# GpSimd's product y and its lower parts of the q and k units, each made as two half-width operations

## The chip, the cores and the metric

The kernel runs on one core of one Trainium2 chip. The core has a matrix engine (TensorE, PE in the profile, with its weight loads as PEld), a vector engine (VectorE, DVE), an activation engine (ScalarE, ACT), GpSimd (POOL), and SyncE (SP), which issues most DMAs. Each engine runs its own instruction list in order, and engines wait for each other through semaphores. The metric is device time in microseconds (us), the median of several runs.

## The reference

Three layers follow each other: attention with a top-32 mask, a gated channel mixer with a causal convolution, and a token mixer with a learned phase. What matters here is the attention:

```python
scores = scale * np.matmul(q, k.transpose(0, 1, 3, 2))      # 4 batches, 8 heads, 576 x 576
kth = np.partition(scores, -32, axis=-1)[..., -32:-31]
mask = scores >= kth
scores = np.where(mask, scores, -1e9)
attn = softmax(scores)                                       # written out in the reference
out = np.matmul(attn, v)                                     # head_dim 64
```

The later layers are matrix products of 512 x 512 and 576 x 576 with elementwise work between them. All is float32.

## The kernel before

**Tiles and steps.** The scores are cut into 144 tiles of 128 query rows by 576 keys. One step of the main loop advances a pipeline of tiles: TensorE makes the scores of a later tile, ScalarE moves them out of PSUM (`scores_out`, L572), VectorE finds the largest 24 of each row (`pick`, eleven short operations on L594, L598, L600), and the 25th to 32nd are found through a product that GpSimd makes.

**The path of y.** For tile i, ScalarE makes n, the sign of each score against the 24th largest (`count`, L607), with its row sum in acc. GpSimd multiplies scores by n into y (`below`, L615, 576 columns) and appends eight numbers made from acc (L616, 8 columns). VectorE takes the eight largest of y (`rest`, L621), and one of them is the threshold in `thrs`. ScalarE makes the exponentials e (`expo`, L202), and VectorE masks, multiplies and sums them in one operation with two SBUF inputs (`mask`, L676, called "the mask" below). The masked tile is then turned by TensorE and multiplied with v.

**Buffers.** There is one buffer for y: y of the next tile waits until L621 has read this one. There are two for n: n of tile i-1 (in step i) needs the buffer that y of tile i-3 (made in the same step) has read.

**q and k units.** For each pair of heads (a unit) ScalarE rounds k and q to the high part (`split_high`, L247), and GpSimd subtracts it to leave the low part (`split_low`, L253): one operation for k over 576 columns, one for q over 576, 320 or 256 columns. DMAs (`double`, L262 to L270) then copy both parts to the places where TensorE reads them.

**Other GpSimd work.** L630 (`nmax`, 6 columns, every third tile), L732 (row sums of a unit), L837 (a sum in the convolution of batches 1 to 3, whose result VectorE needs on L845), L415 (low parts of the later layers, here X, G and L), L354 (weights). On VectorE, L340, L341 and L335 belong to the weights, and L415 makes low parts there too.

**What sets the order.** VectorE and ScalarE run in the order in which the Python code records their work (`FIXED`, `manual_schedule`): one step records the names of `STEP` in turn, among them `rest`, `below`, `pick`, `mask`. The lists of TensorE, GpSimd and SyncE are ordered by the framework's scheduler, which works from its own estimates.

Of the kernel before, what the change touches and what calls it, by code (L numbers as in the profile page):

```python
# [11 lines left out]
F32 = mybir.dt.float32  # L12
# [5 lines left out]
ALU = mybir.AluOpType  # L18
# [72 lines left out]
def mixer(ctx, tc, qT, kT, vt, w_val, conv_t, w_out, w_theta, w_tok, w_ch, out, flag):  # L91
    nc = tc.nc
    safe = flag is None
    P = 128
    B, S, DM = vt.shape
# [97 lines left out]
    s_tiles, s_psum, groups, xT, gate, W, ms = {}, {}, {}, {}, {}, {}, {}  # L193
    owed = [0.0]
    jobs, later, mid, extras, chains, flowing, fill = [], [], [], [], [], [], []
# [21 lines left out]
    def columns_of(t, x):  # L217
        return slice(*COLS[x]) if t == "q" and x is not None else slice(0, S)
# [30 lines left out]
    def split_low(u, x):  # L249
        for t in "kq":  # L250
            high, low = raws[t, u, x]
            c = columns_of(t, x)
            nc.gpsimd.tensor_tensor(low[:, c], low[:, c].bitcast(F32), high[:, c].bitcast(F32), ALU.subtract)  # L253

    def double(u, j, x):

# [320 lines left out]
    def group(i):  # L577
        g, k = divmod(i, G)
        if g not in groups:
            d = {}  # L580
            for nm, shape in (("cand", [P, G, 8 * NSUB]), ("tops", [P, G, K if safe else KC])):
                d[nm] = wk.tile(shape, F32, tag=nm, name=f"{nm}_{g}", bufs=2 if nm == "cand" else 3)
            groups[g] = d
        return groups[g], k
# [26 lines left out]
    def below(i):  # L611

        d, k = group(i)
        y = wk.tile([P, S + NK], F32, tag="y", name=f"y_{i}")
        nc.gpsimd.tensor_tensor(y[:, :S], s_tiles[i], d.pop(("n", k)), ALU.mult)  # L615
        nc.gpsimd.tensor_tensor(y[:, S:], steps, d.pop(("acc", k)).broadcast_to([P, NK]), ALU.subtract)  # L616
        d["y", k] = y

# [653 lines left out]
    for k, part in enumerate(order):  # L1272
        i0 = part["tiles"][0].i
        u, x = part["u"], part["x"]
        split = u // NP in SPLIT
        if k < 2:
            at(-1, lambda u=u: fetch(u, (nc.sync, nc.sync if u else nc.scalar)))
            for j in range(2):
                at(j if k else -1, lambda u=u, j=j: direct(u, j))
        elif split or x == 0:  # L1280
            when = (i0 - 7, i0 - 5, i0 - 5, i0 - 4, i0 - 3) if split or i0 and order[k - 1]["x"] and order[k - 1]["u"] // NP in SPLIT else (i0 - 9, i0 - 8, i0 - 7, i0 - 6, i0 - 3)
            a = (u, x if split else None)
            for step, do in zip(when, (load_heads, split_high, split_low, *(
                    lambda u, x, j=j: double(u, j, x) for j in range(2)))):
                at(max(step, 0), lambda do=do, a=a: do(*a))
        if split or x == 0:
            at(i0 + VAT[0 if split else 1], lambda part=part: load_v(part))
# [58 lines left out]
    def work_1(i):  # L1346
# [13 lines left out]
        "convert": convert,  # L1360
        "pick": lambda i: i <= N and (by_group(i, group_of) if safe else pick(i)),
        "below": lambda i: None if safe else inside(i - 3, below),
        "scores_out": lambda i: i + AHEAD - 1 in s_psum and scores_out(i + AHEAD - 1),
        "turn_out": lambda i: inside(i - LAG - TO - 1, turn_out),
# [65 lines left out]
```

## Time and profile before

| | us |
|---|---|
| median of 3 runs | 820.15 (819.28 to 820.51) |
| the profiled execution: its own time | 818.77 |
| the profiled execution: span of its instructions | 817.0 |

| engine | busy us of the span | instructions |
|---|---|---|
| TensorE matmuls | 722.8 (88%) | 4478 |
| VectorE | 665.9 (82%) | 2708 |
| ScalarE | 633.6 (78%) | 1517 |
| GpSimd | 451.4 (55%) | 557 |

Busy time of an engine counts an operation from its start to its end as the profile records them, also where it stands still in between. The chain of waits is made by going back from the last instruction, at each step to what released it or to the instruction ahead of it on its engine. It tells which engine held the end at which moment.

### The profile page before, as it was taken

The numbers are of one execution on the slowest core, as the hardware profiler recorded it, in microseconds if no ns is written. First come the engines' busy times: TensorE is split into PE (matmuls) and PEld (weight loads), VectorE is DVE, ScalarE is ACT, GpSimd is POOL, SyncE is SP. The second block draws the span as 40 slices with busy tenths as digits, with TensorE's granted clock in tenths as the row PEclk, the third lists the DMA queues.
The fourth block names the chain that finished last, engine by engine and source line by source line (L and its number), as shares of the span: only waits on it lengthen the run. The fifth ranks groups of instructions, "written<-read, shape, count | busy, mean of one in ns | idle before, by whom it ended". The sixth has DMA issues, their size and how long they took to land.

```text
span 817.0 us, 15416 instructions
## 1 busy us (share of the span) xinstructions
PE 722.8 (88%) x4478; PEld 580.9 (71%) x4478; DVE 665.9 (82%) x2708; ACT 633.6 (78%) x1517; POOL 451.4 (55%) x557
## 2 busy tenths in 40 slices
PE   5467899958999899996989989999999899999995
PEld 3345577536757676965787767788988677898995
DVE  5999999879977899997999799989988795353522
ACT  6788999889779888998789988889988874346411
POOL 5977676556644454657577445647895251015500
PEclk9998999989999999998889999999999999999998
DMA  5676776545342343276365523325662300070002
GB/s 153 169 181 167 188 185 173 153 112 137 77 129 72 78 145 91 61 221 174 91 182 159 170 75 87 73 73 145 181 185 79 104 16 1 1 244 21 2 1 63
DMA packets 69982, 94.33 MB, mean 115 GB/s; under 512 B 13312, under 2 KB 36736, under 8 KB 69888
## 3 DMA queue, kind: packets, MB, share of 16 engines
q1 hardware_dynamic: 69568, 92.82, 41.7%
q8 instruction: 38, 0.62, 0.3%
q14 instruction: 56, 0.46, 0.2%
q10 hardware_dynamic: 320, 0.43, 0.2%
HBM read 49.96 MB, written 13.11 MB: 77 GB/s over the span
## 4 chain that ended last, share of the span: by engine, by line
PE 43%; DVE 30%; ACT 13%; POOL 6%; DMA 4%; issue 3%; SPq 1%; ACTq 0%; POOLq 0%; DVEq 0%
PE px L780 7%; PE py L1134 7%; DVE cand L594 6%; DVE s L676 5%; DVE thrs L621 4%; PE pval L529 4%; PE px2t L529 4%; PE pth L529 4%; PE ph L529 4%; PE py L1153 3%; PE pt L689 3%; DVE gp L845 2%; DVE cand L600 2%; PE ps L558 2%; DVE tops L598 2%
## 5 line engine op out<-in xcount | busy, mean ns | idle before, releaser
L615 POOL TENSOR_TENSOR y<-s,n 128x576 f32<-128x576 f32 x144 | 188.6, 1309 | 191.9 <-DVE thrs L621 139.4
L594 DVE MAX8 cand<-s 128x8 f32<-128x96 f32 x864 | 210.2, 244 | 6.1 <-ACT s L572 6.1
L676 DVE SCALAR_TENSOR_TENSOR s<-s,thrs,e 128x576 f32<-128x576 f32 x144 | 140.8, 978 | 2.3 <-ACT e L202 2.3
L607 ACT ACTIVATE n<-s,tops 128x576 bf16<-128x576 f32 x144 | 112.0, 778 | 32.0 <-POOL y L615 13.5
L572 ACT ACTIVATE s<-ps 128x256 f32<-128x256 f32 (+1 forms) x288 | 103.4, 405 | 25.3 <-PE ps L693 9.3
L1134 PE MATMUL py<-w_tok,z 128*128 128x256 f32 (+1 forms) x432 | 116.1, 408 | 6.4 <-DVE z L990 6.4
L621 DVE MAX8 thrs<-y 128x8 f32<-128x584 f32 x144 | 109.3, 759 | 5.4 <-POOL y L616 4.8
L202 ACT ACTIVATE e<-s,least 128x576 f32<-128x576 f32 x144 | 110.8, 769 | 1.4 <-POOL gp L837 1.3
L689 PE MATMUL pt<-ident,s 128*128 128x128 f32 x576 | 95.1, 286 | 16.9 <-ACT pT L708 8.0
L689 PEld LDWEIGHTS pt<-ident,s 128*128 128x128 f32 x576 | 69.8, 146 | 43.1 <-ACT pT L708 14.7
L558 PE MATMUL ps<-kh_None,q 128*128 128x256 f32 x240 | 91.9, 390 | 5.5 <-ACT rb L759 2.8
L1134 PEld LDWEIGHTS py<-w_tok,z 128*128 128x128 f32 x432 | 77.4, 190 | 26.4 <-DVE z L990 8.8
L708 ACT COPY pT<-pt 128x512 f32<-128x512 f32 x128 | 73.1, 571 | 23.2 <-PE pt L689 13.5
L780 PE MATMUL px<-pT,v 128*64 128x256 f32 (+1 forms) x512 | 76.6, 435 | 13.4 <-ACT pT L708 13.4
L598 DVE MAX8 tops<-cand 128x8 f32<-128x48 f32 x432 | 82.6, 191 | 0.1
L559 PE MATMUL ps<-kl_None,q 128*128 128x256 f32 x240 | 71.8, 302 | 0.0
L780 PEld LDWEIGHTS px<-pT,v 128*64 128x64 f32 x512 | 34.3, 143 | 44.2 <-ACT pT L708 15.7
L558 PEld LDWEIGHTS ps<-kh_None,q 128*128 128x128 f32 x240 | 46.8, 195 | 20.1 <-ACT s L572 6.5
L558 PE MATMUL ps<-kh,q 128*128 128x256 f32 (+1 forms) x80 | 36.0, 457 | 22.2 <-ACT s L572 9.3
L600 DVE MATCH_REPLACE8 cand<-tops,cand 128x48 f32<-128x48 f32 x288 | 55.0, 191 | 0.0
L559 PEld LDWEIGHTS ps<-kl_None,q 128*128 128x128 f32 x240 | 47.4, 198 | 2.3 <-issue 0.5
L697 ACT COPY pT<-ps 64x128 f32<-64x128 f32 (+1 forms) x160 | 39.1, 245 | 11.9 <-PE ps L693 5.6
(206 smaller groups left out, 1716.3 us busy)
## 6 DMA issues: line engine op xcount, KB each, us to landing
kh_None<-kh_None SPq DMA_DIRECT2D x48, 144.0 KB, 2.7
kl_None<-kl_None SPq DMA_DIRECT2D x48, 144.0 KB, 2.8
v<-in_vt_dram SPq DMA_DIRECT2D x20, 256.0 KB, 3.7
out_dram<-x2T SPq DMA_DIRECT2D x16, 256.0 KB, 2.9
w<-ch SPq DMA_DIRECT2D x16, 256.0 KB, 4.4
w<-theta SPq DMA_DIRECT2D x16, 256.0 KB, 5.4
raw_hi<-in_w_tok_dram SPq DMA_DIRECT2D x7, 512.0 KB, 3.9
kh<-kh SPq DMA_DIRECT2D x24, 144.0 KB, 2.4
```

The source lines that it names most:

```text
L202: ins = nc.scalar.activation(out, src, func, **more).ins
L529: nc.tensor.matmul(ps[o : o + n], x, y, start=(i + k == 0), stop=(i == last and k == len(ways) - 1), skip_group_check=(n < P))
L558: nc.tensor.matmul(bank[:, :w], q2, kh[:, lo:hi], start=(j == js[0]), stop=False)
L559: nc.tensor.matmul(bank[:, :w], q2, kl[:, lo:hi], start=False, stop=(j == js[-1]))
L594: nc.vector.max(d["cand"][:, k, 8 * x : 8 * x + 8], s_tiles[i][:, x * SUB : (x + 1) * SUB])
L607: nc.scalar.activation(n, s_tiles[i], AF.Sign, bias=d["tops"][:, k, KC - 1 : KC], scale=-(1.0 + 2.0 ** -22), accum_out=acc)
L615: nc.gpsimd.tensor_tensor(y[:, :S], s_tiles[i], d.pop(("n", k)), ALU.mult)
L621: nc.vector.max(thrs[:, N - 1 - i : N - 1 - i + NK], d.pop(("y", k)))
L676: nc.vector.scalar_tensor_tensor(p, p, thr(i), e.exp, ALU.is_ge, ALU.mult, accum_out=part["sums"][:, e.slot : e.slot + 1])
L689: nc.tensor.transpose(e.pt[:, c, :], p[:, c * P : (c + 1) * P], ident)
L780: nc.tensor.matmul(px[d, :], of_v, pT[:, k, :], start=(c == 0), stop=(c == NF), skip_group_check=True)
L1134: nc.tensor.matmul(ps, z[:, m * P : (m + 1) * P], W["tok"][:, w, lo:hi], start=(i + k == 0), stop=(i == NF))
```

## The change

Both products of GpSimd are cut in the middle of their columns and recorded as two operations behind each other. Nothing else is edited.

```diff
         for t in "kq":
             high, low = raws[t, u, x]
             c = columns_of(t, x)
-            nc.gpsimd.tensor_tensor(low[:, c], low[:, c].bitcast(F32), high[:, c].bitcast(F32), ALU.subtract)
+            mid = (c.start + c.stop) // 2
+            for c in (slice(c.start, mid), slice(mid, c.stop)):
+                nc.gpsimd.tensor_tensor(low[:, c], low[:, c].bitcast(F32), high[:, c].bitcast(F32), ALU.subtract)
...
         y = wk.tile([P, S + NK], F32, tag="y", name=f"y_{i}")
-        nc.gpsimd.tensor_tensor(y[:, :S], s_tiles[i], d.pop(("n", k)), ALU.mult)
+        n = d.pop(("n", k))
+        for c in (slice(0, S // 2), slice(S // 2, S)):
+            nc.gpsimd.tensor_tensor(y[:, c], s_tiles[i][:, c], n[:, c], ALU.mult)
         nc.gpsimd.tensor_tensor(y[:, S:], steps, d.pop(("acc", k)).broadcast_to([P, NK]), ALU.subtract)
```

144 operations on y become 288, and 36 on units become 72. The lists of TensorE, VectorE and ScalarE keep their order. GpSimd's list keeps its order too, with the halves next to each other, but for three places, and SyncE's list has one pair of DMAs exchanged (a copy of a high q part now ahead of the copy of a low k part, in the unit of the second place below). Line numbers from L253 on grow by 2, and those behind L615 by 4.

GpSimd's list of the kernel before at about 137 us of its trace: y of one tile, the two low parts of a unit, then the eight columns that finish y.

```order
L354 TENSOR_TENSOR w_tok<-raw_hi_130 128x512
L615 TENSOR_TENSOR y_1964<-s_1678,n_1850 128x576
L253 TENSOR_TENSOR kl_None<-kl_None,kh_None 128x576
L253 TENSOR_TENSOR ql_None<-ql_None,qh_None 128x576
L616 TENSOR_TENSOR y_1964<-steps,acc_1849 128x8
L630 TENSOR_SCALAR least<-tops_1781 128x6
```

The same place of GpSimd's list in the changed kernel:

```order
L356 TENSOR_TENSOR w_tok<-raw_hi_130 128x512
L619 TENSOR_TENSOR y_2008<-s_1716,n_1891 128x288
L255 TENSOR_TENSOR kl_None<-kl_None,kh_None 128x288 x2
L255 TENSOR_TENSOR ql_None<-ql_None,qh_None 128x288 x2
L619 TENSOR_TENSOR y_2008<-s_1716,n_1891 128x288
L620 TENSOR_TENSOR y_2008<-steps,acc_1890 128x8
L634 TENSOR_SCALAR least<-tops_1821 128x6
```

The second half of y stands behind the whole unit now; before, all 576 columns stood ahead of it.

GpSimd's list of the kernel before at about 373 us: a unit whose k part stands ahead of the y of a tile and whose q part behind it.

```order
L616 TENSOR_TENSOR y_4943<-steps,acc_4883 128x8
L253 TENSOR_TENSOR kl_None<-kl_None,kh_None 128x576
L615 TENSOR_TENSOR y_4992<-s_4735,n_4925 128x576
L616 TENSOR_TENSOR y_4992<-steps,acc_4924 128x8
L253 TENSOR_TENSOR ql_None<-ql_None,qh_None 128x576
```

The same place in the changed kernel:

```order
L620 TENSOR_TENSOR y_5046<-steps,acc_4985 128x8
L255 TENSOR_TENSOR kl_None<-kl_None,kh_None 128x288
L619 TENSOR_TENSOR y_5096<-s_4835,n_5028 128x288 x2
L620 TENSOR_TENSOR y_5096<-steps,acc_5027 128x8
L255 TENSOR_TENSOR kl_None<-kl_None,kh_None 128x288
L255 TENSOR_TENSOR ql_None<-ql_None,qh_None 128x288 x2
```

Only the first half of the k part stands ahead of y now. The third place is at about 433 us, where two operations L (L415, 512 columns) stood behind y: now the first of them stands between the halves of y.

## Rows read from the trace of the kernel before

**Rows 1.** The page: busy time by engine, and the chain's shares by engine.
```profile
PE 722.8 (88%) x4478; PEld 580.9 (71%) x4478; DVE 665.9 (82%) x2708; ACT 633.6 (78%) x1517; POOL 451.4 (55%) x557
PE 43%; DVE 30%; ACT 13%; POOL 6%; DMA 4%; issue 3%; SPq 1%; ACTq 0%; POOLq 0%; DVEq 0%
```

**Rows 2.** Busy time by stretch: stretch, its us, then PE, PEld, DVE, ACT, POOL, clock, DMA.
```profile
285.00:420.00 135.00, 122.88 (x806) 98.90 (x802) 126.12 (x536) 116.18 (x292) 83.22 (x105) 0.94 0.48 136
```

**Rows 3.** One line's instructions, L676 (the mask): count, ns minimum/median/maximum, first and last start.
```profile
L676 DVE SCALAR_TENSOR_TENSOR s<-s,thrs,e x144: 784/806/2041, 25.8 to 687.0; 128x576 f32<-128x576 f32 x144
```

**Rows 4.** Instructions in order of time (start us, us, engine line operation): one tile.
```profile
318.89 1.27 POOL L615 TENSOR_TENSOR y<-s,n 128x576 f32<-128x576 f32 x1 [1.20 <-DVE cand L594]
320.13 0.20 POOL L616 TENSOR_TENSOR y<-steps,acc 128x8 f32<-128x8 f32 x1
320.30 0.80 DVE L676 SCALAR_TENSOR_TENSOR s<-s,thrs,e 128x576 f32<-128x576 f32 x1
...
321.03 0.76 DVE L621 MAX8 thrs<-y 128x8 f32<-128x584 f32 x1
```

**Rows 5.** Instructions in order of time: a mask and a unit on GpSimd.
```profile
335.90 1.43 POOL L253 TENSOR_TENSOR kl_None<-kl_None,kh_None 128x576 fp32r<-128x576 f32 x1
335.91 2.04 DVE L676 SCALAR_TENSOR_TENSOR s<-s,thrs,e 128x576 f32<-128x576 f32 x1
337.29 1.95 POOL L253 TENSOR_TENSOR ql_None<-ql_None,qh_None 128x576 fp32r<-128x576 f32 x1
```

**Rows 6.** Instructions in order of time: GpSimd's L837 and VectorE's L845, which needs it.
```profile
306.69 1.41 POOL L837 TENSOR_TENSOR gp<-gp,ct 128x576 f32<-128x576 f32 x1
...
308.64 0.81 DVE L845 SCALAR_TENSOR_TENSOR gp<-xT,w_conv,gp 128x576 f32<-128x576 f32 x1
```

**Rows 7.** Instructions in order of time: a mask that begins while y runs.
```profile
403.19 1.30 POOL L615 TENSOR_TENSOR y<-s,n 128x576 f32<-128x576 f32 x1
...
403.34 1.77 DVE L676 SCALAR_TENSOR_TENSOR s<-s,thrs,e 128x576 f32<-128x576 f32 x1
...
404.45 0.72 POOL L616 TENSOR_TENSOR y<-steps,acc 128x8 f32<-128x8 f32 x1
404.53 0.78 ACT L607 ACTIVATE n<-s,tops 128x576 bf16<-128x576 f32 x1 [0.24 <-POOL y L615]
```

**Rows 8.** The chain of waits in order of time (start us, us, what): masks.
```profile
97.59 1.76 DVE s L676 x2
...
335.99 1.96 DVE s L676 x2
...
414.51 1.42 DVE s L676 x2
420.81 1.87 DVE s L676 x2
...
434.39 1.58 DVE s L676
...
548.37 1.96 DVE s L676 x2
```

**Rows 9.** The chain of waits: first and last of the ten pieces of y.
```profile
14.57 1.26 POOL y L615
...
592.92 1.24 POOL y L615
```

**Rows 10.** Waits of ScalarE: who, for whom, us in total, times, longest us.
```profile
ACT n L607 <- POOL y L615: 13.5, 12, 3.2
...
ACT n L607 <- POOL y L616: 9.7, 9, 2.6
```

**Rows 11.** Instructions in order of time at two of the places where GpSimd's order changes.
```profile
138.16 1.40 POOL L253 TENSOR_TENSOR kl_None<-kl_None,kh_None 128x576 fp32r<-128x576 f32 x1
...
141.48 0.78 ACT L607 ACTIVATE n<-s,tops 128x576 bf16<-128x576 f32 x1
...
376.33 0.77 DVE L621 MAX8 thrs<-y 128x8 f32<-128x584 f32 x1 [0.93 <-POOL y L616]
```

## The prediction

> **What bounds the kernel now.** I read the page first: TensorE, VectorE and ScalarE are all busy for 78 to 88% of the span, and GpSimd for 55% [rows 1]. No engine alone is the limit, so a sum of busy times decides nothing. The chain of waits says who held the end: TensorE 43% of the span, VectorE 30%, ScalarE 13%, GpSimd 6% [rows 1]. Then the stretches: from 285 to 420 us VectorE is busy 126.1 of 135 us with TensorE close behind at 122.9 [rows 2]. What shortens VectorE there is nearly a gain, what shortens it elsewhere mostly not.
>
> Then I read how GpSimd gets at this. The mask on VectorE (L676) takes 0.81 us at the median, but up to 2.04 [rows 3]. In the long case GpSimd's k part had begun 0.01 us ahead: it ran to 337.33, and the mask ended 0.62 us behind that, at 337.95. The q part, next on GpSimd's list, took 1.95 us, though it is as wide as the k part, which took 1.43 [rows 5]. So a VectorE operation with two SBUF inputs and a GpSimd operation do not work at once. The one that comes later stands until the other is done, and the waiting mask got its turn between two GpSimd operations. A mask that begins in the middle of y stands in the same way (1.77 us), and the eight columns behind that y then wait for the mask (0.72 instead of 0.20) [rows 4, 7]. The short searches of `pick` have one input and run beside y undisturbed.
>
> In the usual tile there is no collision. y starts at 318.89, the eight columns at 320.13, the mask at 320.30, undisturbed with 0.80 us [rows 4]. So the eight columns start 0.17 us ahead of the mask. Whatever GpSimd has next starts about when the mask does, and small differences decide who goes first: in rows 5 the k part won by 0.01 us.
>
> **What the change costs on GpSimd.** y takes 1.27 us for 576 columns and the eight columns 0.20 [rows 4]: (1.27 - 0.20)/568 is 1.9 ns a column, with 0.18 us fixed. A half then takes 0.18 + 288 x 1.9 ns = 0.73 us. The next operation starts 0.03 us before the last one's end (318.89 + 1.27 against 320.13), so two halves hold GpSimd for 2 x 0.70 = 1.40 instead of 1.24 us. In rows 5 the overlap is 0.04; I take **+0.14 us a tile**. For units, 1.43 us for 576 columns [rows 5] gives 2.2 ns a column and again 0.14 us for each operation that is cut. The bounds: at 2.2 ns a column, the halves of y would hold GpSimd for about 1.5 us, +0.26; if the fixed part ran wholly beside the operation ahead, nothing would be added. A gain is excluded, as no column is saved. I take the middle, since the row of eight columns shows the fixed part nearly bare. Of the 144 x 0.14 = 20 us for y and 36 x 0.14 = 5 us for units, nearly all lies in GpSimd's idle time.
>
> The Trainium skill (GPSIMD Engine Reference, Instruction dispatch) puts the dispatch of an instruction at tens of cycles, which at 1.2 GHz would be some 0.04 us (an estimate). By that nothing much would move and the sum would come out near 816.5; the row of eight columns with 0.20 us speaks against it.
>
> **What 0.14 us moves.** The eight columns now start about 0.03 us ahead of the mask instead of 0.17, still first, and what stands behind them comes 0.14 us later and so behind the mask. The mask should bear the eight columns, which end 0.17 us after its start: where y or a longer operation ended that late the traced masks kept their 0.80 us, and 0.18 us of an undisturbed mask lie ahead of its 576 columns (0.80 less the 0.62 that it still takes once it is let in [rows 5]). The gains, each against a free mask of 0.73 us on the chain (320.30 to 321.03 [rows 4]):
> - Three masks behind a k part (335.99, 420.81, 548.37 [rows 8]) stood for 1.23, 1.14 and 1.23 us. The k part, which began 0.00 to 0.08 us ahead of them, loses now: 3.6 us. Its consumers are DMAs for a later unit, so its own 0.5 us are hidden.
> - The mask at 414.51 stood 0.69 us behind G [rows 8], which also comes later now: 0.7 us.
> - The mask at 434.39 [rows 8] stood 0.85 us behind L. That L now begins in front of y's second half, about 0.55 us earlier, so the stall falls to about 0.4: 0.45 us.
> - The mask at 97.59 [rows 8] stood 1.03 us behind y. It now gets in after a half: 0.7 us less.
> - At 376 us L621 waited 0.93 us for a y that stood behind a whole k part [rows 11]. Now a half is ahead of it, 0.7 us less, of which the second cut-in of the mask takes some: 0.5 us. SyncE's exchanged pair of copies belongs to this unit; the k copies wait longer, but none of the chain's pieces here is a DMA.
> - Seven more masks stand behind y for some 0.57 us more than behind a half [rows 7], but none of these is a VectorE piece of the chain. Of 4 us I take an eighth, 0.5 us.
>
> Together **6.5 us**. The costs on the path:
> - Ten pieces of y [rows 9] and five of units are on the chain: 15 x 0.14 = 2.1 us.
> - L837 loses against the mask as the k part does, but there VectorE gains nothing: its next operation L845 needs L837. From rows 5, an operation that waits ends 1.29 us behind the mask (339.24 against 337.95), so L837 would end at 306.70 + 0.80 + 1.29 = 308.79 and L845 start at about 308.85 instead of 308.64 [rows 6]. Four such pieces are on the chain: 0.8 us.
> - ScalarE's n waited 21 times for y, 23 us in all [rows 10]. Each wait grows by 0.14, 2.9 us; ScalarE and GpSimd hold a fifth of the chain, so 0.6 us.
> - At 138 us y's second half now stands behind the unit. The unit starts 0.55 us earlier (137.6), its four halves take 4 x 0.74 us, then y's half 0.7: 141.3, and some 1 us for VectorE's turns between them, 142.3. The n that needs it started at 141.48 [rows 11]: 0 to 0.8 us, I take 0.4.
>
> Together **3.9 us**, so the forecast is **2.6 us less**: 816.2 for the profiled execution (818.77, of which 1.8 us lie around the span), and 820.15 - 2.6 = **817.5 us** against the median of the runs shown, which is 1.4 us above the profiled one. Its own range, with the width cost from 0.05 to 0.17 and half or all of the gains on the path, is 815 to 819.5.
>
> **The rivals.**
> *The eight columns come too late (slower).* If the two halves add more than 0.17 us, the upper part of my bounds, the eight columns start behind the mask. They then wait as in rows 7 and end about 0.9 us after the mask's start, while L621 starts 0.73 us after it in tiles with nothing between (320.30 to 321.03 [rows 4]). Fifteen tiles have this spacing, so 15 x 0.2 = 3 us of VectorE, and the width cost at 0.26 adds some 1.8 us to the terms above: -2.6 + 4.8 gives 822.3. For it speaks that the margin is 0.03 us, against it the fixed part read from the short row. Chance 0.21.
>
> *The halves act as one (about the same).* The change would not do what it says if VectorE got no turn between two halves that have no wait between them. The gains that rest on a turn fall away (0.7, 0.5 and 0.5 us), those that rest on the shift stay: 819.2. The turn between the k and the q part in rows 5 speaks against it. The Trainium skill bears on this from both sides: SBUF — State Buffer (two separate sides) has the shared ports held for a whole instruction, by which the forecast stands; GPSIMD Engine Reference (Instruction dispatch) says that each of GpSimd's cores starts the next instruction once its own share is done, by which the ports might never come free between halves, and the time would be 819.2. Chance 0.12.
>
> *y pays for the turns (about the same).* Where the mask cuts in, y's second half ends some 0.65 us later, and an n that starts 0.04 us behind y (404.53 against 404.49 [rows 7]) is pushed by that. At eight places that is 5.2 us of ScalarE; if half of it lands on the end, 817.5 + 2.6 = 820.1. For it: y is on the chain ten times. Against it: L616 waited for the mask at these places already. Chance 0.13.
>
> *The stalls count in full (faster).* If VectorE's saved stalls off the chain also count (4 us instead of 0.5) and the width cost hides, the time is 817.5 - 5 = 812.5. TensorE, busy 91% of rows 2, speaks against it. Chance 0.11.
>
> **How the numbers follow.** The forecast has 0.43. Faster by over 0.2% (1.6 us, about what a measurement of this kernel can tell from no change): most of the forecast's case, 0.38, the full gain, 0.11, and a little of the others: 0.53. Slower: 0.21 and a little more, 0.22. The same: 0.25. The range leaves out the far end of the full gain and the worse half of the slow case: 813 to 822.5.
>
> **What would show it.** Right: halves of 0.70 to 0.76 us; eight columns that start 0 to 0.06 us ahead of an undisturbed mask; no mask of 2 us behind a k part; VectorE's busy time down by 8 to 14 us and GpSimd's up by some 25; L845 waiting for L837. Wrong: halves over 0.76 us with eight columns of 0.7 us in most tiles and L621 waiting for them (the slow case); masks that stand for a whole y of two halves (no turn); masks fast but n waiting much more than 23 us for y (y pays). What breaks the sum most easily is the race at the mask's start, which hundredths of a microsecond decide.

## The result, and the profile after

The changed kernel takes **827.9 us** (median, 825.83 to 828.38) against 819.72 us for the kernel before: a ratio of 1.0094, 95% interval 1.0074 to 1.0113. It is 8 us slower. The forecast was 817.5 us with a range up to 822.5, so both the sign and the range were wrong. The granted clock of TensorE does not explain it: it was 0.959 to 0.973 in the runs of the changed kernel and 0.953 to 0.972 in 17 runs of the kernel before.

The profiled execution took 827.73 us, with a span of 825.8. The page's busy times and chain shares, which answer to [rows 1]:

```profile
PE 720.7 (87%) x4478; PEld 580.0 (70%) x4478; DVE 653.9 (79%) x2708; ACT 633.2 (77%) x1517; POOL 495.7 (60%) x737
...
PE 44%; DVE 20%; ACT 15%; POOL 11%; DMA 5%; issue 3%; SPq 1%; ACTq 0%; POOLq 0%
```

VectorE did get its relief: 12.0 us less busy, and its share of the chain fell from 30 to 20%. GpSimd is busy 44.3 us more, and its share rose from 6 to 11%. Where the relief came from shows in the mask. First its row in the kernel before, from the groups by line (busy us, mean ns, then the idle time before it), then that of the changed kernel, then the changed kernel's y halves and mask as instructions of one line (count, ns minimum/median/maximum; the mask answers to [rows 3]):

```profile
L676 DVE SCALAR_TENSOR_TENSOR s<-s,thrs,e 128x576 f32<-128x576 f32 x144 | 140.8, 978 | 2.3 <-ACT e L202 2.3
```
```profile
L680 DVE SCALAR_TENSOR_TENSOR s<-s,thrs,e 128x576 f32<-128x576 f32 x144 | 125.3, 870 | 2.4 <-ACT e L202 2.4
```
```profile
L619 POOL TENSOR_TENSOR y<-s,n x288: 720/733/1282, 14.5 to 685.5; 128x288 f32<-128x288 f32 x144
...
L680 DVE SCALAR_TENSOR_TENSOR s<-s,thrs,e x144: 790/806/1804, 26.5 to 695.7; 128x576 f32<-128x576 f32 x144
```

The masks together take 15.5 us less; 19 of them were longer than 1.6 us, now one is. That is the change working as it was meant to. The waits for GpSimd show what it cost (who, for whom, us in total, times, longest us), the kernel before first, then the changed one; the two rows of n answer to [rows 10]:

```profile
DVE gp L845 <- POOL gp L837: 6.8, 2, 4.9
...
DVE thrs L621 <- POOL y L616: 4.8, 5, 1.5
```
```profile
ACT n L609 <- POOL y L619: 37.7, 31, 3.7
...
DVE thrs L625 <- POOL y L620: 16.4, 16, 2.1
...
DVE gp L849 <- POOL gp L841: 13.5, 7, 5.0
...
ACT n L609 <- POOL y L620: 0.9, 1, 0.9
```

VectorE's threshold waits 11.6 us more for y's eight columns and its L849 6.7 us more for L841; together more than the masks saved. The two are not alike. The five new waits for L841 (1.3 us each) stand right behind masks that stood for 2.0 us before and take 0.8 now: there a stall only became a wait, and L849 starts 0.14 to 0.17 us later against the mask ahead of it, about what y has become longer. The waits for the eight columns come in other tiles.

Where in the program this happens is seen by setting the start of each of the 144 masks in one trace against its start in the kernel before (us later; worked out from the traces; the last two columns are the experiments y_busy and y_calm below):

```
mask, start before   changed   y in halves in    y in halves in
                      kernel    58 busy tiles     86 calm tiles
  6     51.7          +1.40       +0.84             +0.17
 41    205.9          +4.23       +2.84             -0.56
 68    335.9          +4.63       +3.05             -0.51
 69    341.3          +3.39       +1.81             -0.50
 72    355.5          +4.83       +3.11             -0.49
 83    403.3          +4.19       +3.43             -0.57
 87    425.3          +2.88       +1.98             -0.58
 88    428.4          +4.71       +3.53             -0.58
110    533.2          +6.41       +5.54             -0.60
143    687.0          +8.71       +7.44             -0.44
```

In 81 of the 144 steps from one mask to the next the changed kernel moves by 0.03 us or less: the usual tile costs nothing. Seventeen steps gain over 0.1 us (11.8 us in all), 41 lose (20.2 us), and a loss mostly follows a gain within a few tiles: 1.24 us won at mask 69 are gone by mask 72, and what was won up to mask 87 is gone at 88.

That last place, read in full. Instructions in order of time (start us, us, engine line operation, idle before it), the kernel before:

```profile
413.02 1.29 POOL L615 TENSOR_TENSOR y<-s,n 128x576 f32<-128x576 f32 x1 [3.64 <-DVE thrs L621]
...
414.43 4.80 POOL L415 TENSOR_TENSOR G<-gp,G 128x320 fp32r<-128x320 f32 x4
...
419.25 1.28 POOL L615 TENSOR_TENSOR y<-s,n 128x576 f32<-128x576 f32 x1
...
420.50 0.20 POOL L616 TENSOR_TENSOR y<-steps,acc 128x8 f32<-128x8 f32 x1
...
420.66 1.40 POOL L253 TENSOR_TENSOR kl_None<-kl_None,kh_None 128x576 fp32r<-128x576 f32 x1
420.74 1.94 DVE L676 SCALAR_TENSOR_TENSOR s<-s,thrs,e 128x576 f32<-128x576 f32 x1
...
422.02 1.93 POOL L253 TENSOR_TENSOR ql_None<-ql_None,qh_None 128x576 fp32r<-128x576 f32 x1
...
423.91 1.29 POOL L615 TENSOR_TENSOR y<-s,n 128x576 f32<-128x576 f32 x1
...
425.15 0.21 POOL L616 TENSOR_TENSOR y<-steps,acc 128x8 f32<-128x8 f32 x1
...
426.05 0.76 DVE L621 MAX8 thrs<-y 128x8 f32<-128x584 f32 x1
```

The same in the changed kernel:

```profile
417.22 1.44 POOL L619 TENSOR_TENSOR y<-s,n 128x288 f32<-128x288 f32 x2 [4.07 <-DVE thrs L625]
...
418.77 4.80 POOL L417 TENSOR_TENSOR G<-gp,G 128x320 fp32r<-128x320 f32 x4
...
423.53 1.41 POOL L619 TENSOR_TENSOR y<-s,n 128x288 f32<-128x288 f32 x2
...
424.24 1.32 DVE L680 SCALAR_TENSOR_TENSOR s<-s,thrs,e 128x576 f32<-128x576 f32 x1
...
424.90 0.71 POOL L620 TENSOR_TENSOR y<-steps,acc 128x8 f32<-128x8 f32 x1
...
425.58 1.56 POOL L255 TENSOR_TENSOR kl_None<-kl_None,kh_None 128x288 fp32r<-128x288 f32 x2
...
427.10 1.57 POOL L255 TENSOR_TENSOR ql_None<-ql_None,qh_None 128x288 fp32r<-128x288 f32 x2
...
428.21 1.07 DVE L680 SCALAR_TENSOR_TENSOR s<-s,thrs,e 128x576 f32<-128x576 f32 x1
...
428.61 1.95 POOL L619 TENSOR_TENSOR y<-s,n 128x288 f32<-128x288 f32 x2
...
430.53 0.20 POOL L620 TENSOR_TENSOR y<-steps,acc 128x8 f32<-128x8 f32 x1
...
430.76 0.77 DVE L625 MAX8 thrs<-y 128x8 f32<-128x584 f32 x1 [1.47 <-POOL y L620]
```

From 413.02 on GpSimd has no gap: y, four parts of G, y, the unit, y. In the kernel before it is through at 425.36, and VectorE, held up by a mask of 1.94 us, comes for that y at 426.05: 0.69 us to spare. In the changed kernel the masks are let in early (1.32 and 1.07 us), but GpSimd's stretch has grown from 12.34 to 13.51 us: five operations are cut, and the turns it gives VectorE show in eight columns of 0.71 and a y of 1.95 us. From one start to the next, each cut operation that met no mask holds GpSimd 0.12 to 0.16 us longer, some 0.7 us for the five; one turn more for VectorE (two here, one in the q part of before) makes the other 0.5. The spare 0.69 us are used up, and VectorE waits 1.47 us for y. Counted from the start of the stretch, the threshold comes 13.54 us later instead of 13.03: in all, this place loses 0.5 us. The mask's stall had been free here, since VectorE had to come back for a y that was not yet made.

### The profile page after: what moved, and what is told of

The parts are those of the page before. It is cut to its first block, busy times and chain, and to the rows that moved or that the text cites. A ratio compares the mean times of both kernels' runs of the same rounds, so it can differ in the third digit from the quotient of the medians.

```text
span 825.8 us, 15599 instructions
## 1 busy us (share of the span) xinstructions
PE 720.7 (87%) x4478; PEld 580.0 (70%) x4478; DVE 653.9 (79%) x2708; ACT 633.2 (77%) x1517; POOL 495.7 (60%) x737
## 4 chain that ended last, share of the span: by engine, by line
PE 44%; DVE 20%; ACT 15%; POOL 11%; DMA 5%; issue 3%; SPq 1%; ACTq 0%; POOLq 0%
PE px L784 7%; PE py L1138 7%; POOL y L619 5%; PE pth L531 4%; PE px2t L531 4%; PE pval L531 4%; DVE cand L596 4%; PE ph L531 4%; PE pt L693 3%; DVE thrs L625 3%; PE py L1157 3%; ACT n L609 3%; DVE s L680 3%; PE ps L560 2%; DVE gp L849 2%
## 5 line engine op out<-in xcount | busy, mean ns | idle before, releaser
L619 POOL TENSOR_TENSOR y<-s,n 128x288 f32<-128x288 f32 x288 | 217.2, 775 | 176.3 <-DVE thrs L625 134.8
L680 DVE SCALAR_TENSOR_TENSOR s<-s,thrs,e 128x576 f32<-128x576 f32 x144 | 125.3, 870 | 2.4 <-ACT e L202 2.4
L693 PEld LDWEIGHTS pt<-ident,s 128*128 128x128 f32 x576 | 69.6, 145 | 43.2 <-ACT pT L712 13.8
L620 POOL TENSOR_TENSOR y<-steps,acc 128x8 f32<-128x8 f32 x144 | 54.2, 376 | 0.0
```

The source lines that it names most:

```text
L619: nc.gpsimd.tensor_tensor(y[:, c], s_tiles[i][:, c], n[:, c], ALU.mult)
L680: nc.vector.scalar_tensor_tensor(p, p, thr(i), e.exp, ALU.is_ge, ALU.mult, accum_out=part["sums"][:, e.slot : e.slot + 1])
L693: nc.tensor.transpose(e.pt[:, c, :], p[:, c * P : (c + 1) * P], ident)
```

## The experiments

The first theory at this point was **U**: the split units make the loss. Its rivals were **Y** (y's halves make it), **O** (the order that changed at three places) and **W** (the bare lateness of y).

**One half of the change each.** Label y_only keeps the first of these two edits, u_only the second:

```
-        nc.gpsimd.tensor_tensor(y[:, :S], s_tiles[i], d.pop(("n", k)), ALU.mult)
+        for c in (slice(0, S // 2), slice(S // 2, S)):
+            nc.gpsimd.tensor_tensor(y[:, c], s_tiles[i][:, c], n[:, c], ALU.mult)
...
-            nc.gpsimd.tensor_tensor(low[:, c], ..., ALU.subtract)
+            for c in (slice(c.start, mid), slice(mid, c.stop)):
+                nc.gpsimd.tensor_tensor(low[:, c], ..., ALU.subtract)
```

> Only y of each tile is made in two halves; the lower parts of the units stay one operation each. The change as a whole lost 8.2 us (819.7 to 827.9). If the loss comes from the split units (theory U: a unit's four short operations in a row on GpSimd give VectorE the port between them, and the y behind them comes late), this kernel is within 2 us of the kernel before, 818 to 822 us, and VectorE's waits for y's eight columns stay near the 4.8 us of before. If it comes from y itself (theory Y: a second half that waits for a turn holds back n and the threshold), it is 825 to 829 us, and those waits are near the 16.4 us of the changed kernel. If it comes from GpSimd's changed order at three places (theory O), of which this kernel has two, some 822 to 825 us. If it is only that every y ends 0.16 us later (theory W), 823 to 827 us.

> Only the lower parts of the q and k units are made in two halves; y stays one operation. Theory U (the units make the loss): 825 to 829 us, with GpSimd's busy time up by over 10 us and VectorE's waits for y's eight columns at 10 us or more. Theory Y (y makes it): 815 to 820 us, since the masks under a unit's lower part, 3.6 us by the prediction's sum, are given back and nothing is lost. Theory O, one of the three places: 820 to 823 us. Theory W: 816 to 820 us.

y_only: 824.84 us against 818.63, ratio 1.0072 (1.0055 to 1.0088). u_only: 819.88 us, 1.0016 (1.0005 to 1.0028). The parts add up, 0.72% and 0.16% against 0.94%. Theory U fell: four fifths of the loss come with y. But u_only has none of the gain that theory Y allowed for, either: it is slower, by 1.3 us, where the prediction had 3.6 us of gain from these masks.

**The order.** Dependences for the scheduler alone hold GpSimd's operations in the order of before at the three places (of each pair the first goes first: y's halves or eight columns of a tile, the k or q part of a unit, the L operations; the third place, which the expectation puts at 415 us, is the one at 433 us):

```
+PINS = ((("y", 30), ("k", 6)), (("q", 6), ("y8", 30)), (("k", 12), ("y", 80)),
+        (("k", 12), ("y8", 80)), (("y", 92), ("L", 0)), (("L", 0), ("y8", 92)))
...
+        tc.add_manual_dep(ins, other.name, mybir.DependencyInfo(
+            mybir.DependencyClass.NoSync, mybir.DependencyReason.SCHED_ONLY), reason="the order of before")
```

> The changed kernel whole, but GpSimd's operations in the order of before (both halves stand where the whole operation stood) at the three places where the change moved them: about 138, 376 and 415 us. Theory O (the order): 818 to 822 us. Theories U, Y and W: 825 to 829 us, at most 2 us below the changed kernel, by the 1.2 us that masks come later at 138 us and what the place at 415 us gives.

828.19 us, ratio 1.0108 (1.0090 to 1.0126), no better than the changed kernel. Theory O fell.

**Lateness alone, first attempt.** One more short operation on GpSimd per tile:

```
         nc.gpsimd.tensor_tensor(y[:, :S], s_tiles[i], d.pop(("n", k)), ALU.mult)
+        nc.gpsimd.tensor_tensor(spare, steps, steps, ALU.subtract)
```

> The kernel before with one more GpSimd operation of eight columns (a difference that nobody reads) between y and its eight columns, in every tile: nothing is split, but the eight columns come about as much later as in the changed kernel, 0.15 to 0.2 us. Theory W (the bare lateness makes the loss): 823 to 828 us. Theories U and Y (the turns between halves make it): 819 to 822 us, because no two operations that share VectorE's port stand behind one another more than before but one short one, and GpSimd's busy time grows only by that operation, some 20 us at 0.2 us each, without longer y.

851.48 us, ratio 1.0397, outside all expectations, and the trace says why. The added operations as one line:

```profile
L617 POOL TENSOR_TENSOR spare<-steps x144: 193/198/852, 3.6 to 72.2; 128x8 f32<-128x8 f32 x144
```

They depend on nothing, so the scheduler put all 144 into the first 72 us. The run does not test lateness. It does show that GpSimd sets the time in that opening: 144 x 0.23 = 33 us of added work, and from mask 10 to the end every mask is 32.0 to 32.7 us late.

That, and the stretch at 413 us, gave theory **G**: where GpSimd works without a gap, the operations that others wait for stand behind it all, and each added operation or granted turn is on the path; elsewhere none is.

**y in halves by kind of tile.** In the trace of the kernel before, y of 58 tiles lies in a stretch of GpSimd without a gap over 0.3 us that also holds another y, a unit or L837; the other 86 stand alone.

```
-        nc.gpsimd.tensor_tensor(y[:, :S], s_tiles[i], d.pop(("n", k)), ALU.mult)
+        for c in (slice(0, S // 2), slice(S // 2, S)) if i in BUSY else (slice(0, S),):
+            nc.gpsimd.tensor_tensor(y[:, c], s_tiles[i][:, c], n[:, c], ALU.mult)
```

> y in two halves only in the 58 tiles whose y, in the kernel before, lies in a stretch of GpSimd without a gap over 0.3 us that also holds another y, a unit's lower parts or L837's product; whole in the other 86 tiles; the units' lower parts whole. Theory G (where GpSimd works without a gap, it is GpSimd that sets the time, so each added operation and each turn it grants VectorE is on the path, and elsewhere nothing of it is): nearly all of the 6.2 us that y's halves cost everywhere, 823 to 825.5 us, 4.5 to 7 above the kernel before. Theory W (every later y costs the same): 58/144 of it, 820.5 to 822.

> The other part: y in two halves only in the 86 tiles whose y stands alone in its stretch, whole in the 58. Theory G: nothing lost, 817 to 819.5 us, and perhaps the 0.7 us won where a mask stood behind a lone y. Theory W: 86/144 of 6.2 us, 821.5 to 823.

y_busy: 825.31 us against 818.6, ratio 1.0069 (1.0050 to 1.0088), all of y_only's 1.0072. y_calm: 818.34 us, 0.9996 (0.9983 to 1.0010), no change. Theory G is right about the place of the loss, and W falls. The page's busy times and the waits, y_busy first:

```profile
PE 726.9 (88%) x4478; PEld 584.1 (71%) x4478; DVE 657.2 (80%) x2708; ACT 633.1 (77%) x1517; POOL 465.2 (56%) x615
```
```profile
ACT n L609 <- POOL y L619: 19.2, 16, 3.7
...
DVE gp L849 <- POOL gp L841: 13.5, 7, 5.0
...
DVE thrs L625 <- POOL y L620: 12.1, 12, 1.7
```

The same of y_calm:

```profile
PE 720.8 (88%) x4478; PEld 579.5 (71%) x4478; DVE 667.9 (82%) x2708; ACT 634.3 (78%) x1517; POOL 477.5 (58%) x643
```
```profile
ACT n L609 <- POOL y L619: 31.3, 30, 3.2
...
DVE gp L849 <- POOL gp L841: 6.9, 2, 4.9
...
DVE thrs L625 <- POOL y L620: 5.8, 6, 1.5
```

y_busy adds 13.8 us to GpSimd's busy time and loses 6.7 us; y_calm adds 26.1 us and loses nothing. So not every added microsecond counts even in the busy tiles. GpSimd holds 10% of y_busy's chain by the page, and 6% of y_calm's, no more than before. Two waits go with the loss: VectorE's for the eight columns (4.8 us before) and its wait for L841 (6.8 us before), of which the second is mostly moved stall, as said above. ScalarE's n waits for y, the eight columns counted in (10.2 and 0.9 us), for 29.4 us in y_busy and 32.2 in y_calm, against 23.2 before: y_calm has 9 us more of that wait and loses nothing by it. Nearly all of VectorE's relief lies in y_busy as well (8.7 us less busy, y_calm 2.0 more): gain and loss come in the same tiles.

**One more operation, nothing cut.** The eight columns are written twice:

```
+        nc.gpsimd.tensor_tensor(y[:, S:], steps, d["acc", k].broadcast_to([P, NK]), ALU.subtract)
         nc.gpsimd.tensor_tensor(y[:, S:], steps, d.pop(("acc", k)).broadcast_to([P, NK]), ALU.subtract)
```

> The kernel before with y's eight columns written twice, one after the other, in every tile: nothing is split, the threshold's release comes 0.16 to 0.2 us later, and GpSimd has one more operation per tile, as with y in halves; but the long operations stay whole, so VectorE wins no more turns than before. If the bare extra work on GpSimd makes the loss, it is like y_only, 823.5 to 826 us. If the turns that VectorE takes between the halves make it, 819 to 821.5.

829.17 us, ratio 1.0127 (1.0106 to 1.0147), above the 823.5 to 826 expected of bare work. The two, from the groups by line:

```profile
L617 POOL TENSOR_TENSOR y<-steps,acc 128x8 f32<-128x8 f32 x144 | 81.1, 563 | 10.8
L616 POOL TENSOR_TENSOR y<-steps,acc 128x8 f32<-128x8 f32 x144 | 37.6, 261 | 0.0
```

The second takes 563 ns on average for 0.2 us of work: a waiting VectorE operation goes ahead of it at the new boundary. So this run does not part work from turns, as I had meant it to; it shows that an added operation with the turn that it gives costs this much without any cut in y.

**Fewer operations on GpSimd.** If GpSimd's count sets the time, taking work off it should pay. Five kernels move something to VectorE:

```
kl_dve:         k part of each unit's lower part:   nc.gpsimd.tensor_tensor -> nc.vector.tensor_tensor
y8_dve:         y[:, S:]:  nc.gpsimd.tensor_tensor -> nc.vector.tensor_scalar(y[:, S:], steps, acc, None, ALU.subtract)
y8_busy_dve:    the same in the 58 tiles alone;     halves_y8_dve: the same in the changed kernel
least_dve:      least:     nc.gpsimd.tensor_scalar -> nc.vector.tensor_scalar
```

> The kernel before with the k part of each unit's lower part on VectorE and the q part on GpSimd as before (both whole): GpSimd has 1.4 us less in each of the 18 units, VectorE 0.7 to 0.8 us more; the orders of TensorE and of the transfers also shift at the units. Theory G for the units (GpSimd sets the time there): 813 to 818 us, faster than before, with VectorE's waits for y's eight columns below 4.8 us. If VectorE sets the time around the units, each k part is on the path less the stall of the mask that it no longer meets: 821 to 828.

> The other way round: the kernel before, nothing split, with one operation fewer on GpSimd per tile. y's eight columns (0.27 us of GpSimd each, 39 us in all) are made by VectorE, right behind the threshold of the tile before, at an estimated 0.07 to 0.1 us each, by its other operations of eight columns: 10 to 14 us more of VectorE. If GpSimd's number of operations sets the time where it works without a gap (theory G), taking one away is worth what adding one cost, 6 to 10 us, less VectorE's part that is on the path, 30% of 10 to 14 us: 811 to 817 us. If what cost was only the place of the cut within y (turns), and not the extra operation, VectorE's part is all that is seen: 820 to 826.

> The same for the 58 tiles alone whose y stands in a busy stretch of GpSimd; the other 86 keep their eight columns on GpSimd. Theory G: all the gain and 58/144 of VectorE's price: 810 to 816 us, below the kernel with all 144. Otherwise 819 to 822.

> The kernel before with the product least (48 operations of six columns, 32.9 us of GpSimd's busy time, most of it standing for VectorE's turns) on VectorE, estimated 0.07 to 0.1 us each, 3 to 5 us. A part of these stand in GpSimd's busy stretches. Theory G: 814 to 818 us. If GpSimd's operations behind y don't matter: 819 to 822.

> The changed kernel (y and the units' lower parts in halves) with the eight columns on VectorE, so that GpSimd has as many operations per tile as before. Theory G (the number of operations and the turns between them are what costs, the halves by themselves give little): back to the kernel before or a little better, 816 to 821 us, and slower than y8_dve by what the halves cost, 4 to 8 us. If the lateness of the threshold alone cost (the eight columns behind the second half): 819 to 823. If the turns inside y and the units cost regardless: 826 to 832.

All five are misses, each slower than the kernel before: kl_dve 840.29 us (ratio 1.0258), y8_dve 890.31 (1.0858), y8_busy_dve 841.3 (1.0267), least_dve 826.27 (1.0075, 1.0056 to 1.0094), halves_y8_dve 859.57 (1.0489). In kl_dve VectorE, which works in order, waits for ScalarE's upper part:

```profile
DVE kl L254 <- ACT kh L247: 19.9, 6, 4.5
```

In y8_dve the eight columns come right behind a threshold, at the moment when GpSimd starts the next y, and stand for the whole of it. In order of time, then as a group:

```profile
450.86 1.35 DVE L616 TENSOR_SCALAR y<-steps,acc 128x8 f32<-128x8 f32 x1
450.90 1.28 POOL L615 TENSOR_TENSOR y<-s,n 128x576 f32<-128x576 f32 x1
```
```profile
L616 DVE TENSOR_SCALAR y<-steps,acc 128x8 f32<-128x8 f32 x144 | 104.2, 724 | 10.3 <-ACT n L607 0.3
```

The group in halves_y8_dve:

```profile
L620 DVE TENSOR_SCALAR y<-steps,acc 128x8 f32<-128x8 f32 x144 | 69.1, 480 | 10.3 <-ACT n L609 0.3
```

Here VectorE is the bound (61% of the chain in y8_dve), and here the change does what it is for: with halves the operation takes 0.48 instead of 0.72 us on average, 35 us less in all, and the kernel is 31 us faster than y8_dve, which has y and the units whole. The runs thus say nothing for or against a lighter GpSimd: what was moved met a new wait, and in all five TensorE's order changed as well, by the traces. least_dve, with 34 us less on GpSimd and 8 more on VectorE, only shows that less busy time on GpSimd is no gain by itself.

**y ahead of the unit.** If the gain at the units is lost because y stands behind the unit's four halves, let y go between the k part and the q part:

```
-            ... (load_heads, split_high, split_low, ...)
+            ... (load_heads, split_high, split_low of k, a step later split_low of q behind the latest y, ...)
```

> The kernel before, nothing split, with a unit's lower part of q moved behind the next tile's y on GpSimd (k's stays where it is): the same operations in another order at about ten of the units; TensorE, VectorE and ScalarE keep theirs. Theory G for the units (a y that stands behind both lower parts is late, and VectorE and ScalarE wait for it there): y comes 1.4 us earlier at those units, 816 to 818.5 us; the 4.8 us for which the threshold waits for y are the bound of the gain. If y's place behind the unit costs nothing in the kernel before: 818.5 to 820.5. If q's lower part then comes too late for its transfers and the scores: above 821.

> The same with the units' lower parts in halves (y whole): only_units measured 1.3 us above the kernel before. Theory G: the masks' gain of some 3 us at the units is kept, since y no longer stands behind four halves and their turns: 814 to 818 us. If the gain was lost elsewhere than to y's wait: 819 to 822.

> The same with the whole change (y and units in halves). Theory G: the part of the loss that lies at the units goes, and the part of the other busy stretches (weights' lower parts, sums for the heads) stays: 821 to 826 us, against 827.9. If the units' order has no part in it: 826 to 829.

> What should be the best of the change by theory G: units in halves with q's part behind y, y in halves only in the 86 calm tiles. 813 to 818 us, below the kernel before. If the halves give VectorE nothing that lasts: 818 to 822.

The kernel called only_units there is u_only. y_first: 824.58 us against 818.83, ratio 1.0059 (1.0036 to 1.0081); y_first_u 822.51, 1.0044 (1.0030 to 1.0057); y_first_after 829.97, 1.0130 (1.0113 to 1.0148); calm_first 823.69, 1.0050 (1.0035 to 1.0065). None brings what theory G expected. y_first lies in the third of its ranges, but not for the reason given there: TensorE's waits for the copies of q are 3.7 and 0.5 us, against 3.6 and 0.4 before. A part of its loss goes with the clock: its two runs at a granted clock of 0.970 and 0.972 took 821.3 us, the four at 0.949 to 0.966 took 823.8 to 825.8. In y_first the unit at [rows 5] looks like this, with the instructions of each engine in order of time:

```profile
337.51 1.43 POOL L254 TENSOR_TENSOR kl_None<-kl_None,kh_None 128x576 fp32r<-128x576 f32 x1
...
342.79 1.44 POOL L254 TENSOR_TENSOR ql_None<-ql_None,qh_None 128x576 fp32r<-128x576 f32 x1
```
```profile
337.51 2.04 DVE L680 SCALAR_TENSOR_TENSOR s<-s,thrs,e 128x576 f32<-128x576 f32 x1
...
342.87 1.97 DVE L680 SCALAR_TENSOR_TENSOR s<-s,thrs,e 128x576 f32<-128x576 f32 x1
```

Back to back the two parts catch one mask [rows 5], apart they catch two. All masks together take 144.5 us instead of 140.8, and at masks 61, 70, 89, 97 and 115 the kernel falls back by 1.1 to 1.2 us each; at four of them (not at 89) the mask ahead stood for 1.9 to 2.0 us behind a q part. So a y ahead of the q part is not to be had for nothing. No version tried beats the kernel before; y_calm is level with it.

## Why the prediction was wrong

**Right.** The size of the edit: halves of 733 ns where 0.73 us were worked out. The usual tile, where the eight columns were to start just ahead of an undisturbed mask:

```profile
320.01 1.42 POOL L619 TENSOR_TENSOR y<-s,n 128x288 f32<-128x288 f32 x2 [0.74 <-ACT s L574]
...
321.39 0.20 POOL L620 TENSOR_TENSOR y<-steps,acc 128x8 f32<-128x8 f32 x1
321.41 0.80 DVE L680 SCALAR_TENSOR_TENSOR s<-s,thrs,e 128x576 f32<-128x576 f32 x1
```

The k part that now loses to the mask of [rows 5] (its first half waits for that mask), and a turn between two halves (the mask begins in y's first half and goes ahead of its second):

```profile
340.54 0.79 DVE L680 SCALAR_TENSOR_TENSOR s<-s,thrs,e 128x576 f32<-128x576 f32 x1
...
340.66 2.10 POOL L255 TENSOR_TENSOR kl_None<-kl_None,kh_None 128x288 fp32r<-128x288 f32 x2
...
344.26 1.96 POOL L619 TENSOR_TENSOR y<-s,n 128x288 f32<-128x288 f32 x2
...
344.65 0.97 DVE L680 SCALAR_TENSOR_TENSOR s<-s,thrs,e 128x576 f32<-128x576 f32 x1
```

VectorE's busy time fell by 12.0 us (8 to 14 expected). The larger gains of the sum came too, for a few tiles: by the steps from mask to mask, 1.24, 0.62 and 1.25 us behind the three k parts and 0.70 at the mask of 414.51.

The Trainium skill (GPSIMD Engine Reference, Instruction dispatch) names tens of cycles for one step of the dispatch. That step alone, by which little would move, is not the whole of the cost here: two halves take 1.42 us where the whole y took 1.27 [rows 4].

**The step that failed** is on the side of the costs: of the 25 us by which the operations of GpSimd were to grow, "nearly all lies in GpSimd's idle time", and 2.1 us were put on the path. For the units the same step reads "Its consumers are DMAs for a later unit, so its own 0.5 us are hidden". I asked who reads the k part, and not what is queued behind it on GpSimd: the next tile's y, for which VectorE comes back. In a stretch without a gap, idle time elsewhere is of no use. By the steps from mask to mask the losses are 20.2 us, against 3.9 us of costs in the sum. y_busy shows it for y: 58 of 144 tiles carry the whole loss of y's halves, and the other 86 none. For the units it is read from the trace at 426 us and from u_only's loss of 1.3 us. By the prediction's own 0.14 us the 58 tiles and the 36 cut operations of the units come to 58 x 0.14 + 5 = 13 us of work; the change lost 8.2.

**The terms.** The ten pieces of y and five of units "on the chain" (2.1 us) were the wrong count, since the chain shows what was last and not what is a little behind it. At 426 us y was not on it, with 0.69 us to spare, and was on it as soon as the stretch grew by 1.17. Of pieces of y longer than 1 us the chain has 9 before and 24 after (20 in y_busy, 12 in y_calm). GpSimd's busy time was to grow by some 25 us and grew by 44.3: beside the wider halves, it stands more often for VectorE's turns (52 of the 144 operations of eight columns take over 0.4 us, 20 before). The 3.6 us for masks behind a k part (3.1 by the steps) were won and given back: u_only, which holds this edit and y whole, lost 1.3 us. The n waits (0.6 us) grew by 15.4 us instead of the 2.9 worked out; y_calm shows that 9 us of such a growth can cost nothing, and what it costs in the busy tiles no run shows. L837 (0.8 us) was right in kind and size: at five places L849 starts 0.14 to 0.17 us later against the mask. It adds nothing of its own to y's width: from the start of the eight columns ahead of it to the start of L845 it is 428.21 to 430.34 before, and 433.07 to 435.21 after, 2.1 us each. The place at 138 us (0.4 us) is settled by pinned: the order has no part.

**The rivals.** "The eight columns come too late" did not happen: in y_calm, made of usual tiles, nothing moved. "The halves act as one" is refuted by the rows at 344.26. "The stalls count in full" fell: the stalls went, the time rose (its terms, 3.5 and 2.1 us, also make 5.6 and not 5). "y pays for the turns" was the true one in kind, with the sign that it shows (y late after VectorE's turns), but I looked for it at the eight places where a mask cuts into y, gave it 2.6 us and set it against the forecast's gain. It went by n, too, whose wait is no price in y_calm; the late y that goes with the loss is the one that VectorE's threshold waits for. Its place is the stretches in which GpSimd is without a gap, and its larger part may not be the turns at all.

**What stays open.** How the 6 us of the busy tiles divide between the fixed time of the added operation and VectorE's turns: double8 mixed the two. By account, y_busy's 13.8 us are 58 x 0.16 = 9 us of longer y and some 5 us of turns, and y_calm, which loses nothing, has 14 and 12. Nor did a run show the unit's part directly: moving y ahead of the q part brought a second stalled mask, and y_first_u, 2.1 us faster than y_first, has an interval that overlaps with it. Theory G said where the loss lies; of its forecasts for other orders and for a lighter GpSimd none came true, so it is no recipe yet for a faster kernel.

## What to carry to other kernels

Before a stall is booked as a gain, look at what its engine comes back for next: if that is still being made on the other engine, the stall was cover, and taking it away makes a wait. An engine that is idle for 45% of the span can still set the time in the stretches where it has no gap: list those first, and put what is added there down as a cost (an upper bound: 13.8 us added cost 6.7 in y_busy), with what is queued behind it and not only with what reads it. Splitting a long operation paid where the waiting engine was the bound (31 us from y8_dve to halves_y8_dve) and cost where the split one had no gap.

## What the runs showed of the hardware

A VectorE operation of eight columns with one SBUF tensor and a per-partition scalar, 0.23 us at its shortest in that run, took 1.35 us behind a GpSimd product that started 0.04 us after it (y8_dve, 450.86); I had priced it at 0.07 to 0.1 us. The six columns of least, with a constant in place of the scalar, took 142 ns on average on VectorE, and none more than 150 (least_dve).

The Trainium skill (SBUF — State Buffer, Who interferes with whom) names a tensor_scalar with one SBUF input among the operations that can contend with GpSimd, when it runs in a mode that uses both ports; y8_dve agrees, though no run shows the mode. The same section has the one that is issued first go ahead; here the product started 0.04 us later by the trace, and went first.

A boundary between two GpSimd operations can be a turn for VectorE even where both are short: 261 ns on average for the first and 563 for the second of two equal operations (double8).
